# Output projection of a fused attention and gated-MLP kernel: where w_in is loaded, how many tiles are held, and which engine makes the low parts

## Chip, cores and metric

The kernel runs on one core of a Trainium2 chip, as one launch. The metric is the time of one execution on the device in microseconds (us). The time before is the median of three runs.

## What is computed

One transformer block in float32 for a sequence of 2048 rows with D = 448 features: an attention with 16 heads of 28 features, then a gated MLP that mixes along the sequence. Both have a layer norm ahead of them whose scale and shift come from a condition vector.

```python
mod = (_silu(c) @ w_mod).reshape(c.shape[0], 6, 1, -1)
sa, ca, ga, sb, cb, gb = ...
h = _layernorm(x) * (1 + ca) + sa
x = x + ga * _A_ref(h, A_wqkv, A_wo)          # softmax attention, then @ wo
h = _layernorm(x) * (1 + cb) + sb
x = x + gb * _B_ref(h, B_w_in, B_w_sp, B_b_sp, B_w_out)
# _B_ref: z = gelu(x @ w_in); z1, z2 = halves of z; z2 = layernorm(z2)
#         g = w_sp @ z2 + b_sp;  return (z1 * g) @ w_out
```

## The kernel before, in words

**Products from a high and a low part.** TensorE (PE) multiplies in float32r. A float32 operand is kept as a high part (a copy to float32r) and a low part (the operand less its high part). A product over 448 rows is eleven matmuls, in the order of `STEPS` (L27 to L29): nine `STEPS_MAIN` over the first 384 rows and two `STEPS_Z` over the last 64, whose high and low parts share slot 6. High parts are made by ScalarE (ACT) or GpSimd (POOL), low parts by `sub` (L70), a subtraction on VectorE (DVE) or POOL.

**The order is written by hand.** `tc.manual_schedule()` (L36) keeps each engine's instructions in the order of the source. Semaphores are put in for data and for the reuse of buffers. A DMA takes one of eight DMA semaphores in turn, and its issue also waits until the earlier DMA on that semaphore has landed. Most DMAs are issued by SyncE (SP).

**Stages.** (1) Norm of x, then q, k and v. q and k go to DRAM as high and low parts. (2) Attention over 256 positions u, 16 for each head (L550 to L562): at each position four score matmuls (`s_mm`, L419) of head u // 16, four matmuls for row maxima (`m_mm`, L388) that run 20 positions ahead, an exponential on ACT, a maximum on DVE, and P times V (`pv_mm`, L434) every second position. Head h reads its rows from the tiles k and q number h % 3 (`kst`, `qst`), which L324 to L329 place in the order k0, q0, q2, k2, q1, k1 with small pads between. Per head `n_copy` to `n_scatter` normalise the output and scatter it by DMA into `OT`, the transposed attention output in `heapD`; `o_split` (L477) splits it. (3) Output projection (L666 to L738), the stage that the change is about. (4) z1: 28 units of eleven matmuls (`z1_unit`, L714). (5) z2, the mixing along the sequence, and the product with w_out.

**The output projection.** `wo_mm` makes tile t (128 rows of the sequence, 16 tiles) of attention @ wo in one PSUM bank. `wo_add` adds it to x on DVE and stores the sum. The last head arrives late: after the last P times V, PE sums its softmax denominators, DVE takes the reciprocal (L680) and multiplies (L681), and eight DMAs scatter the result (L471, one row block and one column quarter each, half issued by SP and half by ACT). Then `o_split(3, qb)` splits column quarter qb of slot 6: ACT makes a high part `zt` (L486), DVE or POOL the low part (L71), ACT the high part in place (L488). Only `STEPS_Z` read slot 6. So PE first does `STEPS_MAIN` of `HELD` = 7 tiles, each held in one of the seven ring banks, and then their `STEPS_Z`. Tile t needs quarter t // 4.

For each group of four tiles follow `h2_stats` (statistics on DVE, `rstd_of` on POOL), `h2_norm` (eight DVE instructions, L638) and `h2_group`, which calls `ln_transpose`: 16 transposes on PE into four ring banks, and per bank two ACT passes (L111 into `hfull`, which has two buffers, and L118) and a low part on POOL (L71). The results, `h2T[g]`, are what z1 reads.

w_in's first half is loaded (L652, L74, L75) after the attention and split by `win_prep` into `w1`: the first two row blocks ahead of the held tiles' `STEPS_Z`, the others behind them, high parts on ACT and low parts on POOL. The x rows of group 0 are loaded ahead of the scatter, those of groups 1 to 3 behind it (L611).

Of the kernel before, what the change touches and what calls it, by code (L numbers as in the profile page):

```python
# [33 lines left out]
def tile_adaln_mha_gmlp(ctx, tc, x, wqkv, wo, w_in, w_spT, b_sp, w_out, cT, w_mod, out):  # L34
# [26 lines left out]
    heapD = dpool.tile([128, 24 * 896], F32R, name="heapD")  # L61
# [6 lines left out]
    wqk = hview(heapD, 14336, 8, 896)  # L68
# [8 lines left out]
    def weight_part(dst, i, raw, hi_eng, lo_eng, zero=True):  # L77

        n = raw.shape[-1]
        h = dst[:, i if i < 3 else 6, :n]  # L80
        if hi_eng is act:
            act.activation(h, raw, AF.Copy)
        else:
            hi_eng.tensor_copy(h, raw)
        if i < 3:
            sub(lo_eng, dst[:, 3 + i, :n], raw, h)
        else:
            sub(lo_eng, dst[0:64, 7, :n], raw[0:64], h[0:64])
            if zero:
                pool.memset(dst[64:128, 7, :n].bitcast(F32), 0.0)  # L90
# [6 lines left out]
    def ln_transpose(xns, full_pool, dsts, scol, bcol, engs, los=(pool,) * 4, mid=None, after=None):  # L97

        tps = []
        for c in range(4):  # L100
            tp = ring.tile([128, 512], F32, name="tp", tag="s")
            tps.append(tp)
            for t in range(4):
                pe.transpose(tp[:, t * 128 : (t + 1) * 128], xns[t][:, c * 128 : (c + 1) * 128], ident)  # L104
# [43 lines left out]

    def load_mod(pair, eng):
# [27 lines left out]
    pool.memset(wqk[64:128, 7, :].bitcast(F32), 0.0)  # L177
# [8 lines left out]
    wu = ring.tile([128, 512], F32, name="wu", tag="s")  # L186
# [16 lines left out]
    def mod_col(*parts):  # L203
        pc = ring.tile([128, 512], F32, name="pc", tag="s")
# [8 lines left out]
    def mod_bc(nm, acc):  # L213
        pc = ring.tile([128, 512], F32, name="pc", tag="s")
# [36 lines left out]
    def v_tiles(*kts):  # L251
        pvs = [ring.tile([128, 512], F32, name="pv", tag="s") for _ in kts]
# [7 lines left out]
    def qk_unit(m, g, mid=None):  # L260
        pq = ring.tile([128, 512], F32, name="pq", tag="s")
# [54 lines left out]
    for g in range(NG):  # L316
# [4 lines left out]
        if g == 3:  # L321
            early.close()
            stk = att.enter_context(tc.tile_pool(name="stk", bufs=1))
            kq = {}  # L324
# [60 lines left out]
    def m_mm(j, kb):  # L385
        h, t = divmod(j, NT)
        mt = ring.tile([128, 512], F32, name="mt", tag="s")
# [13 lines left out]
    def m_fin(h):  # L401
        mx = mxs.pop(h)
        tp = ring.tile([128, 512], F32, name="mtp", tag="s")
# [12 lines left out]
    def s_mm(u, qb):  # L416
        h, kt = divmod(u, NT)
        st = ring.tile([128, 512], F32, name="st_ps", tag="s")
# [43 lines left out]
    def n_scatter(h):  # L462
        o = osb.pop(h)
        a, e = h * DH, (h + 1) * DH
        while a < e:
# [3 lines left out]
            for qb in range(4):  # L469
                for (sl, r), eng in zip(dests, (sp, act if h == H - 1 else sp)):  # L470
                    eng.dma_start(  # L471
# [30 lines left out]

    LEAD = 20
# [21 lines left out]
    for i in range(4):  # L525
        at(120 + 8 * i, wo_load, i)
        at(124 + 8 * i, wo_prep, i)

# [44 lines left out]
    w2 = hview(heapD, 14336, 8, 896)  # L573
    uT = hview(heapD, 14336, 14, 512)
# [5 lines left out]
    wraw = fh.tile([128, 4, 896], F32, name="wraw", tag="heapE")  # L580
# [41 lines left out]
    def h2_stats(g):  # L622
        mv3[g] = t3.tile([128, 4, 2], F32, name="mv3"), t3.tile([128, 4], F32, name="rs3")
        sts = []
        for tt in range(4):
# [3 lines left out]
        for tt in range(4):  # L629
            dve.bn_aggr(out=mv3[g][0][:, tt, :], in_=sts[tt])  # L630
        rstd_of(mv3[g][0][:, :, 1], mv3[g][1], 4)

    def h2_norm(g):
        mv, rs = mv3.pop(g)
# [9 lines left out]
    def win_load(half, i, p=None):  # L644
        if half == 0:
            raw = wraw[:, i, :]
        else:
            raw = p.tile([128, 896], F32, name="raw_in", bufs=1)
        raw_in[half, i] = raw
        c0 = half * FH  # L650
        if i < 3:
            sp.dma_start(raw, w_in[i * 128 : (i + 1) * 128, c0 : c0 + FH])  # L652
        else:
            load_z(sp, raw, w_in[384:448, c0 : c0 + FH])

    def win_prep(half, i, lo_eng):
        weight_part((w1, w2)[half], i, raw_in.pop((half, i)), act, lo_eng)
# [6 lines left out]


# [5 lines left out]
    HELD = 7  # L671
    x_load(0)
    for i in range(4):
        win_load(0, i)
# [8 lines left out]
    for g in range(1, 4):  # L683
        x_load(g)
    for i in range(2):
        win_prep(0, i, pool)
    for t in range(1, HELD):
        wo_mm(t, STEPS_MAIN)
    for qb in range(4):
        o_split(3, qb, dve if qb % 2 == 0 else pool)  # L690
    for i in range(2, 4):
        win_prep(0, i, pool)
    for t in range(HELD):
        wo_mm(t, STEPS_Z)
        wo_add(t)
    h2_stats(0)
    wo_tile(7)
    h2_stats(1)
    h2_norm(0)
    stg.close()  # L700
# [4 lines left out]
    def h2_group(g):  # L705
# [4 lines left out]
        ln_transpose(xns, t3b, h2T[g], cols["cb"], cols["sb"], (act,) * 4)  # L710
# [3 lines left out]
    def z1_unit(g, f):  # L714
        ps_t = ring.tile([128, 512], F32, name="z1_ps", tag="s")
# [20 lines left out]
    h2_stats(3)  # L736
    win_load(1, 0, t3)
    win_load(1, 1, t3b)  # L738
    for g in range(NG):
        for f in range(7):  # L740
            z1_unit(g, f)
            if g == 0 and f == 0:
                h2_norm(3)
            if g == 0 and f in (1, 5):
                h2_group(2 + f // 5)
            if g == 1 and f in (3, 5):
                win_prep(1, f // 4, dve)
                win_load(1, 2 + f // 4, (t3, t3b)[f // 4])
# [23 lines left out]
    def z2_gemm(t):  # L772
# [3 lines left out]
        for hf in range(2):  # L776
            ps_t = ring.tile([128, 512], F32, name="z2_ps", tag="s")
# [42 lines left out]
    def mix_part(tb, st, f):  # L820
        hi, lo = wsp[tb, st]
        if st == 0:
            acc[f] = ring.tile([128, 512], F32, name="acc", tag="s")
# [118 lines left out]
```

## Time and profile before

| what | value |
|---|---|
| median of three runs (lowest to highest) | 1466.33 us (1465.02 to 1467.49) |
| time of the profiled execution | 1466.46 us |
| span of the profiled execution | 1464.7 us |
| granted TensorE clock, mean | 0.999 |
| first matmul of the output projection (L599) | 895.78 us |
| first matmul of z1 (L717) | 941.29 us |
| DMA, mean over the span | 76 GB/s |

Times within the profile are us from the start of the span. A row of the timeline has the start, the length, the engine, the line, the operation, its operands and the count of instructions merged into it; in brackets stands how long the engine was idle before it and what ended that. A row of the windows has, for each stretch, its length and the busy time and count of instructions on PE, PEld (weight loads), DVE, ACT and POOL, then the granted PE clock, the busy share of the DMA engines and their rate. A matmul's busy time is longer than its distance to the next one, because matmuls are pipelined: before a stall the last one is still shown as busy when PE could have issued the next.

### The profile page before, as it was taken

What the parts mean: (1) busy time and instruction counts of PE and PEld (TensorE: products, weight loads), DVE (VectorE), ACT (ScalarE), POOL (GpSimd) and SP (SyncE); (2) the same over time, 40 slices, a digit from 0 to 9 for tenths busy, and PEclk for the clock granted to TensorE, in tenths of its full rate; (3) what the DMA queues carried; (4) which work ended last, traced back from release to release, by engine and by line L of the source; (5) the groups of instructions that cost most, each with busy time, mean ns of one, the idle gap of its engine ahead of it and who ended that gap; (6) DMA issues with size and microseconds to landing.
All of it is one profiled execution on the core that took longest, in us unless ns stands there. A gap on an engine that the chain in (4) does not pass through costs nothing.

```text
span 1464.7 us, 19637 instructions
## 1 busy us (share of the span) xinstructions
PE 1436.5 (98%) x7314; PEld 1015.3 (69%) x7314; DVE 884.6 (60%) x1440; ACT 733.1 (50%) x1390; POOL 302.0 (21%) x273
## 2 busy tenths in 40 slices
PE   5899999999999999999999999999999999999999
PEld 5787755555555555555555555888988888888887
DVE  6557888888888888888888832921552411413114
ACT  3523577677677767767776786442432211211111
POOL 6734200000002011001000021520763400302002
PEclk9999999999999999999999999999999999999999
DMA  7554401221022211221012004442002321313223
GB/s 220 146 163 151 145 9 46 52 49 43 15 52 53 53 39 40 53 51 41 21 47 52 11 19 139 151 149 101 8 14 99 119 77 67 113 64 106 84 69 107
DMA packets 56133, 111.24 MB, mean 76 GB/s; under 512 B 11901, under 2 KB 22781, under 8 KB 53517
## 3 DMA queue, kind: packets, MB, share of 16 engines
q1 hardware_dynamic: 55868, 109.76, 25.1%
q8 instruction: 57, 0.93, 0.3%
q10 hardware_dynamic: 168, 0.23, 0.1%
q14 instruction: 40, 0.32, 0.1%
HBM read 75.89 MB, written 29.48 MB: 72 GB/s over the span
## 4 chain that ended last, share of the span: by engine, by line
PE 92%; DVE 2%; POOL 2%; DMA 2%; issue 1%; ACT 0%; SPq 0%; ACTq 0%; DVEq 0%; POOLq 0%
PE st_ps L419 18%; PE mt L388 16%; PE o_ps L434 16%; PE acc L825 7%; PE acc L827 7%; PE acc L826 7%; PE z_ps L779 5%; PE z_ps L717 5%; PE pq L265 4%; PE y_ps L866 2%; PE y_ps L865 2%; PE y_ps L867 2%; PE pv L256 1%; PE tp L104 1%; POOL heapD L71 1%
## 5 line engine op out<-in xcount | busy, mean ns | idle before, releaser
L393 DVE TENSOR_REDUCE pm<-mt 128x1 f32<-128x512 f32 x1024 | 632.0, 681 | 121.8 <-PE mt L388 121.4
L423 ACT ACTIVATE P<-st_ps 128x512 f32<-128x512 f32 x1024 | 514.2, 618 | 154.3 <-PE st_ps L419 153.9
L419 PE MATMUL st_ps<-qst,kst 86*128 86x512 f32 x1024 | 409.8, 411 | 0.0
L388 PE MATMUL mt<-kst,qst 84*128 84x512 f32 x1024 | 406.6, 397 | 0.3 <-DVE pm L393 0.3
L419 PEld LDWEIGHTS st_ps<-qst,kst 86*128 86x128 f32 x1024 | 193.1, 189 | 144.8 <-issue 82.2
L434 PE MATMUL o_ps<-P,V 128*32 128x512 f32 x2048 | 247.5, 598 | 0.0
L388 PEld LDWEIGHTS mt<-kst,qst 84*128 84x128 f32 x1024 | 194.8, 190 | 38.3 <-DVE pm L393 0.7
L71 DVE TENSOR_TENSOR wsp_l<-raw_sp,wsp_h 128x512 fp32r<-128x512 f32 x64 | 53.7, 841 | 185.7 <-ACT wsp_h L762 185.7
L762 ACT ACTIVATE wsp_h<-raw_sp 128x512 fp32r<-128x512 f32 x64 | 40.3, 631 | 229.1 <-DMA raw_sp<-in_w_spT_dram 187.3
L434 PEld LDWEIGHTS o_ps<-P,V 128*32 128x32 f32 x2048 | 54.1, 109 | 123.5 <-issue 116.6
L71 POOL TENSOR_TENSOR heapD<-u,heapD 128x512 fp32r<-128x512 f32 x27 | 44.7, 1692 | 254.0 <-ACT heapD L844 170.2
L460 POOL TENSOR_TENSOR osb<-osb,rb 128x512 f32<-128x512 f32 x15 | 19.2, 1281 | 349.6 <-DMA rb<-r_scr 192.0
L265 PE MATMUL pq<-heapD 128*128 128x512 f32 x308 | 85.8, 396 | 2.9 <-DVE heapD L71 2.9
L825 PE MATMUL acc<-wsp_h,heapD 128*128 128x512 f32 x224 | 87.6, 391 | 0.6 <-DVE u L842 0.6
L827 PE MATMUL acc<-wsp_h,heapD 128*128 128x512 f32 x224 | 87.3, 390 | 0.0
L826 PE MATMUL acc<-wsp_l,heapD 128*128 128x512 f32 x224 | 87.2, 389 | 0.0
L265 PEld LDWEIGHTS pq<-heapD 128*128 128x128 f32 x308 | 58.0, 189 | 16.4 <-DVE heapD L71 3.4
L71 POOL TENSOR_TENSOR nl<-nf,nh 16x128 fp32r<-16x128 f32 x16 | 7.2, 453 | 285.5 <-issue 152.3
L267 ACT ACTIVATE qf<-pq 128x512 f32<-128x512 f32 x28 | 16.7, 597 | 70.1 <-PE pq L265 70.1
L870 DVE TENSOR_TENSOR x2t<-x2t,y_ps 128x448 f32<-128x448 f32 x12 | 7.5, 622 | 72.9 <-PE y_ps L867 72.9
L825 PEld LDWEIGHTS acc<-wsp_h,heapD 128*128 128x128 f32 x224 | 42.1, 188 | 9.7 <-DVE u L842 1.4
L71 POOL TENSOR_TENSOR ql<-qf,qh 128x512 fp32r<-128x512 f32 x28 | 36.4, 1304 | 59.7 <-ACT qh L269 47.2
(150 smaller groups left out, 1693.3 us busy)
## 6 DMA issues: line engine op xcount, KB each, us to landing
raw_sp<-in_w_spT_dram SPq DMA_DIRECT2D x64, 256.0 KB
kst<-qk_scr SPq DMA_DIRECT2D x45, 224.0 KB
qst<-qk_scr SPq DMA_DIRECT2D x45, 224.0 KB
qk_scr<-qh SPq DMA_DIRECT2D x28, 256.0 KB
qk_scr<-ql SPq DMA_DIRECT2D x28, 256.0 KB
z_scr<-z1t SPq DMA_DIRECT2D x28, 256.0 KB
z<-z_scr SPq DMA_DIRECT2D x28, 256.0 KB
wm<-in_w_mod_dram SPq DMA_DIRECT2D x12, 392.0 KB
```

Of the source, the lines that this page charges most:

```text
L71: eng.tensor_tensor(out=dst, in0=a, in1=hi.bitcast(F32), op=ALU.subtract)
L265: pe.matmul(pq, wqk[:, b, m * 128 : (m + 1) * 128], hT[g][:, a, :], start=j == 0, stop=j == NST - 1)
L388: pe.matmul(mt, qst[h % 3][0:84, t * 128 : (t + 1) * 128], kst[h % 3][0:84, kb * 512 : (kb + 1) * 512], start=True, stop=True)
L393: dve.tensor_reduce(out=pms[h][:, t, kb : kb + 1], in_=mt, axis=AX.X, op=ALU.max)
L419: pe.matmul(st, kst[h % 3][0:86, kt * 128 : (kt + 1) * 128], qst[h % 3][0:86, qb * 512 : (qb + 1) * 512], start=True, stop=True)
L423: act.activation(p, st, AF.Exp, scale=SCALE)
L434: pe.matmul(otile[h][32 * qb : 32 * qb + 32, :], V[:, kt, h, :], ptiles.pop((u, qb)), start=kt == 0, stop=kt == NT - 1)
L717: pe.matmul(ps_t, w1[:, b, f * 128 : (f + 1) * 128], h2T[g][:, a, :], start=j == 0, stop=j == NST - 1)
L779: pe.matmul(ps_t[:, :D], h2T[g][:, a, tt * 128 : (tt + 1) * 128], w2[:, b, hf * D : (hf + 1) * D], start=j == 0, stop=j == NST - 1)
L825: pe.matmul(acc[f], z2[st][:, 0, fs], hi, start=st == 0, stop=False)
L826: pe.matmul(acc[f], z2[st][:, 0, fs], lo, start=False, stop=False)
L827: pe.matmul(acc[f], z2[st][:, 1, fs], hi, start=False, stop=st == NT - 1)
```

## The change

1. **w_in's first half is loaded during attention.** `heapD` is cut into 20 rows and a separate tile `heapF` of 4 rows at the same address. `heapF` first holds the upper half of `wqk`, then `wraw` (the raw w_in), then the upper halves of `w2` and `uT` (class `Halves`). The loads are issued at positions 180, 188, 196 and 204. All four `win_prep` stand ahead of the held tiles, and all four x loads ahead of the scatter.
2. **Eight held tiles.** Tile 7 (and 15) takes the bank of `ps_o` in place of a ring bank.
3. **The last splits on DVE**, all four, two of them between the adds; three of the eight scatters are issued by ACT and five by SP.
4. **Order after the splits.** Tiles 8 to 12 come before the first group's transposes, 13 and 14 between the two groups, 15 after the second. The low parts of all four groups are on DVE in place of POOL. The third group's four statistics stand between the second group's low parts. Groups 2 and 3 follow the 5th and the 10th z1 unit (they followed the 2nd and the 6th).
5. **k and q tiles** are placed in the order k0, q0, k1, q1, k2, q2 without pads. By the built program their first bytes lie in the partition at 54336, 62528, 70784 (q2), 78976 (k2), 87200 (q1) and 95424 (k1) before, and at 54080 and each 8192 bytes on after.

`bank(...)` is the ring allocation under a shorter name, and `:n` became `0:n`; neither changes an instruction.

```diff
-    heapD = dpool.tile([128, 24 * 896], F32R, name="heapD")
+    heapD = dpool.tile([128, 20 * 896], F32R, name="heapD")
+    heapF = dpool.tile([128, 4 * 896], F32R, name="heapF", tag="heapF")
...
-            for i, (nm, pad) in enumerate((("k0", 64), ("q0", 0), ("q2", 16), ("k2", 0), ("q1", 8), ("k1", 8))):
-                if pad:
-                    stk.tile([128, pad], F32, name=f"pad{i}")
-                kq[nm] = stk.tile([128, S], F32R, name=f"{nm[0]}st{nm[1]}")
-            kst, qst = ([kq[f"{n}{i}"] for i in range(3)] for n in "kq")
+            kq = [[stk.tile([128, S], F32R, name=f"{n}st{i}") for n in "kq"] for i in range(3)]
+            kst, qst = [a[0] for a in kq], [a[1] for a in kq]
...
-                for (sl, r), eng in zip(dests, (sp, act if h == H - 1 else sp)):
-                    eng.dma_start(
+                for (sl, r), i in zip(dests, (2 * qb, 2 * qb + 1)):
+                    (act if h == H - 1 and i in (1, 3, 6) else sp).dma_start(
...
+        at(180 + 8 * i, win_first, i)
...
-            wo_ps[t] = ring.tile([128, 512], F32, name="wo_ps", tag="s")
+            wo_ps[t] = bank("wo_ps") if t % 8 < 7 else ps_o.tile([128, 512], F32, name="wo_ps", tag="o")
...
-    HELD = 7
-    x_load(0)
+    HELD = 8
+    for g in range(4):
+        x_load(g)
     for i in range(4):
-        win_load(0, i)
+        raw_in[0, i] = wraw[0][:, i, :]
+        win_prep(0, i, pool)
...
-    for g in range(1, 4):
-        x_load(g)
-    for i in range(2):
-        win_prep(0, i, pool)
     for t in range(1, HELD):
         wo_mm(t, STEPS_MAIN)
-    for qb in range(4):
-        o_split(3, qb, dve if qb % 2 == 0 else pool)
-    for i in range(2, 4):
-        win_prep(0, i, pool)
-    for t in range(HELD):
+    o_split(3, 0, dve)
+    o_split(3, 1, dve)
+    for t in range(4):
         wo_mm(t, STEPS_Z)
         wo_add(t)
+    o_split(3, 2, dve)
+    for t in range(4, 8):
+        wo_mm(t, STEPS_Z)
+        wo_add(t)
+    o_split(3, 3, dve)
     h2_stats(0)
-    wo_tile(7)
     h2_stats(1)
     h2_norm(0)
...
-        ln_transpose(xns, t3b, h2T[g], cols["cb"], cols["sb"], (act,) * 4)
+        ln_transpose(xns, t3b, h2T[g], cols["cb"], cols["sb"], (act,) * 4, (dve,) * 4, None, after)
...
-    for t in (8, 9, 10):
+    for t in range(8, 12):
         wo_tile(t)
     h2_norm(1)
-    wo_tile(11)
-    h2_group(0)
-    h2_stats(2)
-    wo_tile(12)
-    wo_tile(13)
+    wo_mm(12, STEPS)
+    wo_add(12)
+    h2_group(0, lambda c: wo_tile(13) if c == 2 else None)
+    wo_tile(14)
+
+    def last_tile(c):
+        if c == 2:
+            wo_tile(15)
+        h2_stats(2, ((0, 2, 1, 3).index(c),))
+
+    h2_group(1, last_tile)
     h2_norm(2)
-    h2_group(1)
-    wo_tile(14)
-    wo_tile(15)
     h2_stats(3)
...
-            if g == 0 and f == 0:
+            if g == 0 and f == 4:
+                h2_group(2)
                 h2_norm(3)
-            if g == 0 and f in (1, 5):
-                h2_group(2 + f // 5)
+            if g == 1 and f == 2:
+                h2_group(3)
```

More of the change, by code (lines that the diff above doesn't have):

```diff
@@ L100, in ln_transpose @@
         for c in range(4):
-            tp = ring.tile([128, 512], F32, name="tp", tag="s")
+            tp = bank("tp")
             tps.append(tp)
@@ L147, in tile_adaln_mha_gmlp, with bank @@
     wms, xts, raws = {}, {}, {}
+    def bank(name):
+        return ring.tile([128, 512], F32, name=name, tag="s")
     def load_mod(pair, eng):
@@ L251, in v_tiles @@
     def v_tiles(*kts):
-        pvs = [ring.tile([128, 512], F32, name="pv", tag="s") for _ in kts]
+        pvs = [bank("pv") for _ in kts]
         for j, (a, b) in enumerate(STEPS):
@@ L386, in m_mm @@
         h, t = divmod(j, NT)
-        mt = ring.tile([128, 512], F32, name="mt", tag="s")
+        mt = bank("mt")
         pe.matmul(
@@ L501, in wo_prep, with win_first @@
         weight_part(wos, i, wo_raw.pop(i), pool, pool)
+    wraw = []
+    def win_first(i):
+        if not wraw:
+            wraw.append(dpool.tile([128, 4, 896], F32, name="wraw", tag="heapF"))
+        if i < 3:
+            sp.dma_start(wraw[0][:, i, :], w_in[i * 128 : (i + 1) * 128, 0:FH])
+        else:
+            load_z(sp, wraw[0][:, 3, :], w_in[384:448, 0:FH])
     LEAD = 20
@@ L620, in wo_add, with h2_stats @@
         sp.dma_start(x2_scr[t * 128 : (t + 1) * 128, :], xt[:, :D])
[L622 to L625, printed above, removed]
+    def h2_stats(g, tts=range(4)):
+        if g not in mv3:
+            mv3[g] = t3.tile([128, 4, 2], F32, name="mv3"), t3.tile([128, 4], F32, name="rs3"), []
+        mv, rs, sts = mv3[g]
+        for tt in tts:
             st = t3.tile([128, 6], F32, name="st3", bufs=4)
```

77 lines of the change are left out of this document (39 added, 38 removed).

## Prediction, made before the changed kernel ran

> **What bounds the kernel now.** I read the page first, then the windows of the stage between attention and z1, then the timeline of PE in it, and last the rows of whatever ended PE's waits.
>
> ```profile
> PE 92%; DVE 2%; POOL 2%; DMA 2%; issue 1%; ACT 0%; SPq 0%; ACTq 0%; DVEq 0%; POOLq 0%
> ```
>
> The chain that ended last is PE for 92% of the span. PE's own matmuls therefore set the time, and an edit helps only where PE waits or where its matmuls come faster.
>
> ```profile
> 895.78:910.00 14.22, 14.10 (x66) 12.13 (x65) 4.70 (x3) 3.56 (x6) 1.97 (x1) 1.00 0.74 223
> 910.00:914.50 4.50, 1.96 (x9) 1.50 (x9) 3.46 (x5) 2.38 (x5) 4.29 (x3) 1.00 0.81 274
> ...
> 926.70:941.30 14.60, 13.05 (x79) 11.86 (x78) 13.91 (x24) 8.49 (x13) 8.07 (x8) 1.00 0.26 95
> 941.30:1015.10 73.80, 73.80 (x342) 61.35 (x341) 19.79 (x29) 33.56 (x52) 15.95 (x14) 1.00 0.36 128
> ```
>
> PE is idle only between 910 and 914.5 (2.54 of 4.50 us) and between 926.7 and 941.3 (1.55 us). From 941.3 on, in z1, it has no gap. The timeline shows the stops one by one:
>
> ```profile
> 898.16 11.72 PE L599 MATMUL wo_ps<-heapD 128*128 128x448 f32 x54
> 910.80 1.88 PE L599 MATMUL wo_ps<-heapD 128*128 128x448 f32 x8 [0.92 <-ACT zt L486]
> 914.42 12.63 PE L599 MATMUL wo_ps<-heapD 128*128 128x448 f32 x61 [1.74 <-POOL heapD L71]
> 926.89 1.91 PE L104 MATMUL tp<-ident,x 128*128 128x128 f32 x16
> ...
> 933.10 0.79 PE L104 MATMUL tp<-ident,x 128*128 128x128 f32 x3
> 935.35 1.64 PE L104 MATMUL tp<-ident,x 128*128 128x128 f32 x13 [1.46 <-DVE x L638]
> 936.75 4.71 PE L599 MATMUL wo_ps<-heapD 128*128 128x448 f32 x22
> 941.29 1.07 PE L717 MATMUL z_ps<-heapB,heapA 128*128 128x512 f32 x4
> ```
>
> Pace: 61 matmuls begin between 914.42 and 926.89, so one takes 0.204 us. Thirteen transposes begin between 935.35 and 936.75, so one takes 0.108 us. With these, PE could have gone on at 898.16 + 54 x 0.204 = 909.18, at 910.80 + 8 x 0.204 = 912.43 and at 933.10 + 3 x 0.108 = 933.42. It went on at 910.80, 914.42 and 935.35. The stops cost 1.62 + 1.99 + 1.93 = **5.5 us**. That is all this stage can give.
>
> **The change part by part.** The first two stops are the wait for the last splits:
>
> ```profile
> 902.23 0.69 DVE L681 TENSOR_TENSOR osb<-osb,rb 128x512 f32<-128x512 f32 x1
> 902.95 3.94 ACTq L471 DMA_DIRECT2D heapD<-osb  x4
> ...
> 907.00 1.80 ACT L82 ACTIVATE heapA<-wraw 128x896 fp32r<-128x896 f32 x2 [10.47 <-DMA heapD<-osb]
> 908.03 4.65 POOL L71 TENSOR_TENSOR heapA<-wraw,heapA 128x896 fp32r<-128x896 f32 x2 [32.86 <-DMA heapD<-osb]
> 908.70 0.61 ACT L486 ACTIVATE zt<-heapD 128x512 fp32r<-128x512 f32 x1
> 909.35 1.35 DVE L71 TENSOR_TENSOR heapD<-heapD,zt 64x512 fp32r<-64x512 f32 x1 [6.43 <-ACT zt L486]
> ...
> 912.76 1.60 POOL L71 TENSOR_TENSOR heapD<-heapD,zt 64x512 fp32r<-64x512 f32 x1
> ```
>
> The second quarter's low part stood on POOL behind two of w1's (until 912.68) and ended at 914.36. In the new order it is on DVE, and w1's work is earlier: ACT's four high parts follow the copy of the last head's output (0.90 us each, from 896.6), POOL's four low parts run from 897.5 at about 2.1 us each, to 906 with the memset.
>
> The price is one collision. DVE's multiply at 902.23 now meets POOL's third low part (901.7 to 903.8). Rows of before show what follows: DVE's low part at 909.35 took 1.35 us on 64 partitions beside POOL, where the multiply took 0.69 us on 128 with POOL idle. So the multiply ends between 902.9 and 904.6, and I take 904.6. The Trainium skill ("SBUF — State Buffer", section "SBUF: two separate sides") calls this an exclusive lock: a DVE instruction with two SBUF inputs waits out a POOL instruction that reads SBUF. The trace agrees: the 1.35 us ended 0.5 us after POOL's first low part. By that rule alone the scatter leaves 1.7 us later, which speaks against the change.
>
> Loading w_in early does not empty the queue ahead of the scatter:
>
> ```profile
> x<-in_x_dram SPq DMA_DIRECT2D x3, 896.0 KB
> ...
> wraw<-in_w_in_dram SPq DMA_DIRECT2D x3, 448.0 KB
> ```
>
> Before, one x load and four row blocks of w_in were ahead (2688 KB, 2.75 MB). After, it is four x loads (3584 KB, 3.67 MB).
>
> ```profile
> 897.60:904.00 6.40, 6.40 (x31) 5.42 (x30) 4.05 (x2) 0.00 (x0) 0.00 (x0) 1.00 1.01 373
> ```
>
> At 373 GB/s from 897.6 the x loads end at 907.4. SP's five scatters follow in the same queue, and three of them wait for the landing of an x load by their semaphores. Before, the first split began 908.70 - 902.95 = 5.75 us after the first issue, partly behind ACT's w1 work. I put the first split at 908.5 to 910.3 and take 909.5. ACT needs 1.2 us for a quarter (0.61 + 0.63), DVE 0.7 us behind the high part. So quarter 0 is ready at 910.8 and quarter 1 at 912.0.
>
> PE has 63 matmuls of held tiles after 898.16 (nine more than before) and reaches `STEPS_Z` at 911.0. Tiles 0 to 3 take 1.6 us, and tile 4 needs quarter 1 at 912.6. So no wait with the value taken, 0.8 us with the first split at 910.3. Both stops (3.6 us) go. Next late is DVE:
>
> ```profile
> 913.26 3.81 DVE L619 TENSOR_TENSOR x<-x,wo_ps 128x448 f32<-128x448 f32 x7
> 916.99 2.20 DVE L627 BATCH_NORM_STATS2 st<-x 128x6 f32<-128x448 f32 x4
> 919.11 0.36 DVE L630 BATCH_NORM_AGGREGATE mv<-st 128x2 f32<-128x6 f32 x4
> ...
> 923.26 3.19 DVE L638 TENSOR_SCALAR x<-x,mv,rs 128x64 f32<-128x64 f32 x8 [0.89 <-POOL rs L95]
> ...
> 927.96 7.34 DVE L638 TENSOR_SCALAR x<-x,mv,rs 128x64 f32<-128x64 f32 x8
> ```
>
> From 911.7 its order is: four adds at 0.54 (2.2), a split (0.7), four adds (2.2), a split (0.7), two statistics (2 x 2.56), a norm (3.19). That ends at 925.8, or 926.2 if the first add is 0.4 late. PE arrives at 898.16 + 134 x 0.204 = 925.5. New wait: 0.3 to 0.7 us, I take **0.5**.
>
> The third stop (1.93) was the second norm, which took 7.34 us beside POOL's low parts against 3.19 us without. With the low parts on DVE, POOL has none here, so I take 3.19. DVE: adds of 8 to 11 until 928.4, norm until 931.6, add 12 until 932.2, then the first low part at 0.69, until 932.9. PE: transposes until 927.9, tiles 13 and 14 until 932.4, then transposes again. Their third bank was ACT's third pass of group 0, whose buffer that first low part frees:
>
> ```profile
> 927.59 0.78 ACT L111 ACTIVATE hfull<-tp,col_sb,col_cb 128x512 f32<-128x512 f32 x1 [10.20 <-PE tp L104]
> 928.40 0.63 ACT L118 ACTIVATE heapB<-hfull 128x512 fp32r<-128x512 f32 x1
> ```
>
> 932.9 + 0.78 = 933.7 against PE's 933.3: new wait 0.4 us. If the low parts cost 1.4 us, as beside POOL, it is 1.1 us. I take **0.7**. Group 0's last low part ends near 936.3, before PE's 937.2. Later DVE has the third group's norm done at about 947.5, where PE, after five z1 units (2.5 us each by the last window above), asks at 949.7. So the later place of groups 2 and 3 costs nothing; without those 2 us it would cost what is missing.
>
> Taken at nothing: the four w_in loads during attention (1.84 MB, 5 us at 373 GB/s, spread over 70 us in which the DMA share is about 0.2, below; if a load holds up m's DMA, that one has ten us to spare). `uT` and `w2` keep their addresses.
>
> **The k and q tiles.** The attention has 64 score matmuls in each of these three stretches, one head each (heads 3, 4 and 5):
>
> ```profile
> 305.73:352.29 46.56, 46.56 (x259) 26.80 (x258) 39.34 (x68) 33.15 (x68) 1.74 (x2) 1.00 0.18 42
> 352.29:398.98 46.69, 46.69 (x258) 26.80 (x257) 39.31 (x68) 33.22 (x69) 1.74 (x2) 1.00 0.17 41
> 398.98:445.48 46.50, 46.50 (x258) 26.70 (x257) 39.29 (x67) 33.12 (x68) 7.27 (x8) 1.00 0.18 42
> ```
>
> PE has no gap in any, yet they differ by up to 0.19 us. The work is the same; the tiles differ. So the place of the tiles may set a few ns per matmul, which no row shows directly. If all 14 full heads ran as the third, 14 x (46.58 - 46.50) = 1.2 us would be gained; if all ran as the second, 14 x 0.11 = 1.5 us lost. Addresses not seen here could go further. I take **0** and keep -3 to +4.
>
> **Sum.** 5.5 us of stops go, 0.5 + 0.7 and 0.2 for the splits come: 1466.46 - 4.1 = 1462.4 us. The median shown is 0.13 below the profiled execution, which gives 1462.3 us.
>
> **Rivals.** (a) *The wait moves to DVE.* Eight low parts join it between 932 and 943. For it: it is busy 13.91 of 14.60 us already. Against: 7.34 us of that is a norm stretched by POOL. If low parts stay at 1.4 us and the norm at 5 us, PE's second transposes start 2 us late: gain 2, 1464.3 us. (b) *The scatter is held by the x loads.* At 274 GB/s (910 to 914.5 above) they end at 911, quarter 0 is ready at 914, PE waits 3 us: gain 1.1, 1465.2 us. Against: the 373 GB/s were on the same queue. (c) *Attention runs faster* with all six tiles at one offset, by 2 us more than nothing: 1460.3 us. (d) *Attention runs slower.* Place: the score and maximum matmuls of 15 heads. Slower than before by over 0.2% needs 4.1 + 2.9 = 7 us, or 0.47 us a head: it decides from 47.05 us a head on, and at 47.1 us (8.2 us) gives 1470.5 us. Against: that is more than twice the spread seen. (e) *It does not do what it says*: w1 still runs when the splits come, and both stops stay: gain 1.9 less 1.2, 1465.6 us. Against: nothing holds ACT's high parts behind the scatter now.
>
> **How the numbers follow.** Forecast 0.47; (a) 0.13; (b) 0.08; (c) 0.17; (d) 0.10; (e) 0.05. The range reaches from (c) with a full gain of 5.5, 1466.3 - 5.5 - 2 = 1458.8, to just over no change, 1467.5, past (a), (b) and (e); only (d) and the far end of (c) stay out. Differences under 0.2%, 2.9 us, can hardly be told from none: faster means below 1463.4. The forecast and its neighbours toward losses of 1 us and more in attention give: faster 0.56, same 0.33, slower 0.11.
>
> **What would show it.** Right: z1's first matmul about 41.4 us after the output projection's first (45.51 before), no idle PE row at the first `STEPS_Z`, short stops of 0.3 to 0.7 us at each group's transposes, the second norm near 3.2 us, and head stretches of 46.4 to 46.8 us. Wrong: a multiply at 902 that takes over 2.5 us, a first `zt` later than 15 us after the first projection matmul, low parts on DVE of 1.3 us and more, or heads at 47 us.

## Result and profile after

The changed kernel takes 1460.75 us (median of 12 runs, 1459.44 to 1465.07). The kernel before, run on the same chip, takes 1465.62 us. The ratio is 0.9969, with a 95% interval of 0.996 to 0.9979. So 4.9 us are gained, where 4.0 had been forecast (1462.3 against 1466.33), and the time lies inside the range of 1458.8 to 1467.5.

The profiled execution after takes 1460.85 us, with a span of 1459.1 us. These are the rows of its timeline that answer to those of before: start, length, engine, line, and in brackets the idle time ahead and what ended it.

```profile
893.39 2.09 PE L618 MATMUL wo_ps<-heapD 128*128 128x448 f32 x9
...
895.06 8.78 POOL L83 TENSOR_TENSOR heapA<-wraw,heapA 128x896 fp32r<-128x896 f32 x4 [22.30 <-ACT heapA L94]
895.77 13.58 PE L618 MATMUL wo_ps<-heapD 128*128 128x448 f32 x63
899.84 2.04 DVE L699 TENSOR_TENSOR osb<-osb,rb 128x512 f32<-128x512 f32 x1
901.90 7.30 SPq L482 DMA_DIRECT2D heapD<-osb  x5
901.90 3.34 ACTq L482 DMA_DIRECT2D heapD<-osb  x3
...
908.54 0.63 ACT L497 ACTIVATE zt<-heapD 128x512 fp32r<-128x512 f32 x1 [11.04 <-DMA heapD<-osb]
910.00 14.63 PE L618 MATMUL wo_ps<-heapD 128*128 128x448 f32 x71 [0.65 <-ACT heapD L499]
...
921.81 3.16 DVE L659 TENSOR_SCALAR x<-x,mv,rs 128x64 f32<-128x64 f32 x8
924.47 2.41 PE L116 MATMUL tp<-ident,x 128*128 128x128 f32 x16
926.64 4.71 PE L618 MATMUL wo_ps<-heapD 128*128 128x448 f32 x22
927.01 3.19 DVE L659 TENSOR_SCALAR x<-x,mv,rs 128x64 f32<-128x64 f32 x8
930.64 1.29 DVE L83 TENSOR_TENSOR heapB<-hfull,heapB 128x512 fp32r<-128x512 f32 x2
931.19 1.91 PE L116 MATMUL tp<-ident,x 128*128 128x128 f32 x16
...
932.85 2.48 PE L618 MATMUL wo_ps<-heapD 128*128 128x448 f32 x11
935.16 1.09 PE L736 MATMUL z_ps<-heapB,heapA 128*128 128x512 f32 x4
```

Read it from the bottom. z1 begins at 935.16, 41.77 us after the first projection matmul at 893.39; before it was 45.51. The stage gave 3.7 us. Of the three stops, one is left, ahead of the first `STEPS_Z` at 910.00. It ends with the splits, whose first instruction, the first `zt`, began at 908.54, 15.15 us behind the stage's start, and had waited for the scatter ("DMA heapD<-osb"). The second norm takes 3.19 us where it took 7.34. DVE's low parts take 0.65 us each (two in 1.29).

The two spans differ by 5.6 us, and not all of that is the change. This table has every profile of the study: the start of the first score matmul, the attention (from there to the first projection matmul), the stage (from there to z1), and the first `zt` behind the stage's start, all in us. The kernel before, next to each, ran on the same chip.

| profile | first score | attention | stage | first zt | median (before) |
|---|---|---|---|---|---|
| before | 167.14 | 728.64 | 45.51 | 12.92 | |
| after | 165.62 | 727.77 | 41.77 | 15.15 | 1460.75 (1465.62) |
| e12_after_again | 166.84 | 727.47 | 41.88 | 15.27 | 1461.82 (1466.29) |
| e1_kq | 165.24 | 727.00 | 45.36 | 12.81 | 1465.17 (1465.53) |
| e6_old_kq | 165.52 | 728.12 | 40.87 | 13.62 | 1461.94 (1466.46) |
| e2_low_pool | 166.84 | 727.17 | 45.72 | 14.92 | 1465.09 (1465.53) |
| e3_mult | 164.14 | 727.34 | 41.75 | 15.15 | 1460.65 (1465.53) |
| e4_x | 164.14 | 727.39 | 40.66 | 12.03 | 1459.52 (1465.53) |
| e11_x_again | 165.37 | 727.77 | 40.14 | 12.04 | 1461.26 (1466.29) |
| e5_x_held7 | 165.20 | 727.49 | 40.66 | 12.03 | 1459.63, one run |
| e8_win_late | 167.82 | 727.18 | 47.75 | 17.20 | 1465.54 (1466.46) |
| e9_held7 | 167.04 | 727.12 | 41.65 | 13.73 | 1462.38 (1466.46) |
| e7_split_pool | 165.10 | 727.43 | 41.42 | 15.05 | 1459.50 (1466.46) |
| e10_stats | 167.81 | 727.73 | 41.42 | 14.82 | 1462.65, one run |

No edit here changes the work ahead of the first score, yet that part spreads from 164.14 to 167.82. The part behind z1's start spreads from 523.4 to 525.2. The same code spreads too: the two profiles of the kernel after differ by 1.22 us ahead of the first score and by 1.0 us behind z1's start. Both spreads are larger than most effects here. Behind z1's start the change moved groups 2 and 3; that shows nothing clear of this spread (523.4 and 525.0 in before and e1_kq, 523.9 and 524.9 in after and e12_after_again). So each edit is read in its own stretch, and the medians serve as a check. What is left of the change: 3.7 us in the stage and, by the mean of the twelve profiles with the new tile order (727.40) against the two with the old (728.38), 1.0 us in the attention. Together 4.7, against 4.9 by the medians.

### The profile page after: what moved, and what is told of

The parts are those of the page before. It is cut to its first block, busy times and chain, and to the rows that moved or that the text cites. A ratio compares the mean times of both kernels' runs of the same rounds, so it can differ in the third digit from the quotient of the medians.

```text
span 1459.1 us, 19621 instructions
## 1 busy us (share of the span) xinstructions
PE 1436.4 (98%) x7314; PEld 1017.5 (70%) x7314; DVE 881.3 (60%) x1458; ACT 732.4 (50%) x1390; POOL 276.3 (19%) x255
## 4 chain that ended last, share of the span: by engine, by line
PE 94%; DVE 3%; DMA 2%; issue 1%; SPq 0%; ACT 0%; POOL 0%; DVEq 0%; ACTq 0%
PE st_ps L430 18%; PE mt L399 16%; PE o_ps L445 16%; PE acc L848 6%; PE acc L850 6%; PE acc L849 6%; PE pq L280 5%; PE z_ps L802 5%; PE z_ps L736 5%; PE pv L271 2%; PE y_ps L889 2%; PE y_ps L888 2%; PE y_ps L890 2%; PE tp L116 1%; PE wo_ps L618 1%
## 5 line engine op out<-in xcount | busy, mean ns | idle before, releaser
L83 POOL TENSOR_TENSOR heapF<-u,heapD 128x512 fp32r<-128x512 f32 x27 | 44.6, 1684 | 256.8 <-ACT heapD L867 256.8
L280 PE MATMUL pq<-heapD 128*128 128x512 f32 x196 | 64.6, 407 | 0.0
L848 PEld LDWEIGHTS acc<-wsp_h,heapD 128*128 128x128 f32 x224 | 42.1, 188 | 10.5 <-DVE u L865 2.3
L850 PEld LDWEIGHTS acc<-wsp_h,heapD 128*128 128x128 f32 x224 | 42.1, 188 | 8.9
L849 PEld LDWEIGHTS acc<-wsp_l,heapD 128*128 128x128 f32 x224 | 42.1, 188 | 8.2
```

The source lines that it names most:

```text
L83: eng.tensor_tensor(out=dst, in0=a, in1=hi.bitcast(F32), op=ALU.subtract)
L280: pe.matmul(pq, wqk[:, b, m * 128 : (m + 1) * 128], hT[g][:, a, :], start=j == 0, stop=j == NST - 1)
L848: pe.matmul(acc[f], z2[st][:, 0, fs], hi, start=st == 0, stop=False)
L849: pe.matmul(acc[f], z2[st][:, 0, fs], lo, start=False, stop=False)
L850: pe.matmul(acc[f], z2[st][:, 1, fs], hi, start=False, stop=st == NT - 1)
```

## Experiments

### Where the k and q tiles lie: e1_kq and e6_old_kq

e1_kq is the kernel before with the new order alone; e6_old_kq is the kernel after with the old order.

```diff
-            kq = {}
-            for i, (nm, pad) in enumerate((("k0", 64), ("q0", 0), ("q2", 16), ("k2", 0), ("q1", 8), ("k1", 8))):
...
+            kq = [[stk.tile([128, S], F32R, name=f"{n}st{i}") for n in "kq"] for i in range(3)]
```

> The kernel before with one part of the change alone: the k and q tiles of attention allocated in their natural order and without the pads between them. In the profiles of before and after, attention (first score matmul to first projection matmul) took 728.64 and 727.77 us, heads 46.50 to 46.73 by head mod 3 before and 46.47 to 46.68 after. Theory: the addresses of these tiles set that difference, so attention takes about 727.8 us here and the time falls by 0.9 us, to about 1464.7. Rival: the addresses do nothing, attention stays at 728.6 within 0.2, the heads keep their pattern by head mod 3, and the time is that of before within 1 us. The idle PE row of 3.0 us at 70.12, which before shows and after does not, tells apart as well: if it is there again, it belongs to the code, if it isn't, to the single execution.

> The kernel after with the k and q tiles of attention back in the order and with the pads of before, the converse of e1_kq. There the natural order alone gave attention (first score matmul to first projection matmul) 727.00 us against before's 728.64, while four profiles with the change's layout gave 727.2 to 727.8. Theory: the addresses of these tiles set attention, so it takes 728.3 to 728.9 us here, with heads that differ by head mod 3, and the time is 1.0 to 1.6 us over after's. Rival: what sets it is another part of the layout or the execution itself: attention stays at 727.0 to 727.8. The projection stage stays at 41.8 by either.

The windows of heads 3, 4 and 5 in e1_kq (length of the stretch, busy time and count on PE, PEld, DVE, ACT and POOL, granted clock, DMA share, GB/s):

```profile
303.45:349.93 46.48, 46.48 (x259) 26.72 (x257) 39.30 (x67) 33.15 (x68) 1.73 (x2) 1.00 0.18 42
349.93:396.41 46.48, 46.48 (x259) 26.72 (x257) 39.30 (x67) 33.15 (x68) 1.73 (x2) 1.00 0.18 42
396.41:442.87 46.46, 46.46 (x258) 26.67 (x257) 39.30 (x68) 33.16 (x68) 7.27 (x8) 1.00 0.18 42
```

The same heads in e6_old_kq:

```profile
303.94:350.45 46.51, 46.51 (x258) 26.80 (x257) 39.30 (x67) 33.12 (x68) 1.73 (x2) 1.00 0.18 42
350.45:397.16 46.71, 46.71 (x258) 26.77 (x257) 39.32 (x68) 33.20 (x69) 1.73 (x2) 1.00 0.18 41
397.16:443.62 46.46, 46.46 (x258) 26.70 (x257) 39.29 (x67) 33.12 (x68) 7.24 (x8) 1.00 0.18 42
```

With the new order the three heads are alike; with the old one the head that works on k1 and q1 is 0.2 us longer, as before. All profiles show it: the heads that work on k1 and q1 (1, 4, 7, 10 and 13) take 46.70 to 46.79 us in the two with the old order and 46.46 to 46.57 in the twelve with the new one. Undoing this one edit brings the pattern back, and applying it alone removes it. So the addresses set it, at about 1 us over the attention (1.6 in e1_kq; 0.7 in e6_old_kq against the mean, less than expected). This is 0.07% of the time, and the interval of e1_kq's ratio, 0.9979 to 1.0002 around 0.999, holds it without showing it. Why an address costs PE 0.2 us in the 258 matmuls of such a head is not settled. The stage of e6_old_kq had been expected at 41.8 and took 40.87, because its scatter landed earlier (below).

### What sets the scatter: e3_mult, e4_x and e11_x_again

e3_mult (the first diff) takes two low parts off POOL while DVE multiplies; e4_x (the second) takes two x loads out of the scatter's way; e11_x_again is e4_x once more.

```diff
-    for i in range(4):
+    for i in range(2):
         raw_in[0, i] = wraw[0][:, i, :]
         win_prep(0, i, pool)
+    for i in range(2, 4):
+        act.activation(w1[:, 2 if i < 3 else 6, :], wraw[0][:, i, :], AF.Copy)
+    pool.memset(w1[64:128, 7, :].bitcast(F32), 0.0)
...
     n_scatter(h)
+    sub(dve, w1[:, 5, :], wraw[0][:, 2, :], w1[:, 2, :])
+    sub(dve, w1[0:64, 7, :], wraw[0][0:64, 3, :], w1[0:64, 6, :])
```

```diff
-    for g in range(4):
+    for g in range(2):
         x_load(g)
...
     n_scatter(h)
+    for g in range(2, 4):
+        x_load(g)
```

> The kernel after, with w1's third and fourth low parts on DVE behind the last head's multiply, so that POOL has done its two when the multiply starts. It takes away what lengthened the multiply (2.04 us after, 0.69 before), not the loads of x ahead of the scatter. Theory A, the multiply sets the scatter: the scatter is issued 1.35 us earlier, the first zt starts at about 13.8 us after the first projection matmul in place of 15.15, PE's stop of 1.38 us ahead of the first STEPS_Z falls to 0.0 to 0.1, and the time falls by 1.3 us. Theory B, the four loads of x fill the DMA engines until about 906.5 and set the scatter: it is issued 1.35 us earlier but lands less than 0.5 us earlier, the stop stays at 0.9 to 1.4 and the time within 0.5 us of after.

> The kernel after, with the loads of x's third and fourth group issued behind the last head's scatter. It takes away the transfers that the scatter shares the DMA engines with, not the length of the multiply. Theory B (loads of x set the scatter's landing): the scatter issued at about 8.5 us after the first projection matmul lands about 2 us behind its issue, the first zt starts at 11.5 to 13 us in place of 15.15, PE's stop of 1.38 us ahead of the first STEPS_Z goes and the time falls by about 1.3 us. Theory A (the multiply sets it): the first zt starts no more than 0.4 us earlier, and the time stays within 0.4 us of after. The tiles of the third group could be late instead: then PE stops at the ninth tile's sum or its bank, at about 28 us.

> e4_x once more, beside the kernel after on the same chip, as the fastest version so far. Theory: the stage takes 40.66 us whatever the transfers do, against 40.7 to 41.8 after (a mean of about 41.4 from the profiles with four loads ahead), so it is 0.5 to 1 us faster than after, within what the early part varies by. Rival: nothing, since the landing mostly comes in time after as well: within 0.3 us.

The timeline of e3_mult, whose stage begins at 891.48:

```profile
897.92 0.69 DVE L702 TENSOR_TENSOR osb<-osb,rb 128x512 f32<-128x512 f32 x1
898.64 8.24 SPq L482 DMA_DIRECT2D heapD<-osb  x5
...
906.63 0.63 ACT L497 ACTIVATE zt<-heapD 128x512 fp32r<-128x512 f32 x1 [11.03 <-DMA heapD<-osb]
908.08 14.62 PE L618 MATMUL wo_ps<-heapD 128*128 128x448 f32 x71 [0.65 <-ACT heapD L499]
```

The multiply is back at 0.69 us and the scatter leaves 1.35 us earlier, 7.16 us into the stage in place of 8.51. The first `zt` still comes at 15.15. The stage is unchanged, 41.75. That is theory B. The timeline of e4_x, whose stage begins at 891.53:

```profile
893.91 28.25 PE L618 MATMUL wo_ps<-heapD 128*128 128x448 f32 x134
897.98 2.04 DVE L699 TENSOR_TENSOR osb<-osb,rb 128x512 f32<-128x512 f32 x1
900.04 4.22 SPq L482 DMA_DIRECT2D heapD<-osb  x5
903.56 0.63 ACT L497 ACTIVATE zt<-heapD 128x512 fp32r<-128x512 f32 x1 [7.91 <-DMA heapD<-osb]
```

Here the multiply is as long as in after, and the scatter leaves at the same 8.51 us. It lands in half the time: `zt` 3.5 us behind the issue in place of 6.6. PE runs all 134 matmuls without a stop. The two kernels part the causes: with four loads ahead, the transfers ahead of the scatter set its landing and the multiply does not. The DMA engines show it as well: in after they are busy for a share of 0.96 and more from 3 to 13 us into the stage, in e4_x the share is down to 0.12 from 7 to 8 us, before the scatter is issued. Another path could be the semaphores that scatters share with x loads, but in after seven of the eight issues follow one another within 3.4 us (8.51 to 11.85), and only the last waits, until 15.07.

On the whole time the repetition gave 1461.26 us, 0.6 below the kernel after on the same chip (ratios to before 0.9964, 0.9951 to 0.9978, and 0.9967, 0.9955 to 0.998). The stage is 1.1 to 1.7 us shorter, but no comparison of medians here can show that, and up to 0.5 of it is PE's pace (last section).

### What the eighth tile covers: e9_held7 and e5_x_held7

e9_held7 is the kernel after with this edit; e5_x_held7 has this edit and that of e4_x.

```diff
-    HELD = 8
+    HELD = 7
...
     for t in range(4, 8):
-        wo_mm(t, STEPS_Z)
+        wo_mm(t, STEPS_Z if t < 7 else STEPS)
```

> The kernel after with seven held tiles in place of eight: the eighth tile's nine main matmuls come behind the splits. Theory: each held tile covers 1.84 us (nine matmuls of 0.204) of the wait for the scatter, so PE's stop ahead of the first STEPS_Z grows from 1.38 to 3.2 us and the stage from 41.8 to 43.6. Rival: the held tile is not the cover, since the same work is done later and some later stop shrinks by it: the stage grows by less than 0.8 us.

> e4_x (the third and fourth x load behind the scatter) with seven held tiles in place of eight. In e4_x the first zt began 12.0 us after the first projection matmul, PE had no stop and the stage took 40.66 us; in e9_held7, with all x loads ahead, the first zt began 13.7 us after it, and PE reached the first STEPS_Z 13.5 us after it and stopped 1.6 us. Theory: what counts is the landing alone: with the split ready 1.45 us behind the zt, at 13.5, seven tiles cover it and the stage is 40.7 to 40.9 us, so that the eighth held tile is a second cure for the same wait. Rival: the eighth tile does more than cover the landing (its bank, or the order of the adds on DVE): the stage is 41.2 us or more, with a stop of 0.4 us or more somewhere behind the splits.

The timeline of e9_held7:

```profile
896.58 11.51 PE L618 MATMUL wo_ps<-heapD 128*128 128x448 f32 x54
...
907.90 0.63 ACT L497 ACTIVATE zt<-heapD 128x512 fp32r<-128x512 f32 x1 [9.62 <-DMA heapD<-osb]
909.35 16.45 PE L618 MATMUL wo_ps<-heapD 128*128 128x448 f32 x80 [1.26 <-DVE heapD L83]
```

The timeline of e6_old_kq, with eight tiles:

```profile
896.02 28.25 PE L622 MATMUL wo_ps<-heapD 128*128 128x448 f32 x134
907.26 0.63 ACT L501 ACTIVATE zt<-heapD 128x512 fp32r<-128x512 f32 x1 [9.51 <-DMA heapD<-osb]
```

These two had nearly the same landing (13.73 and 13.62 us), earlier than after's. With eight tiles PE does not stop; with seven it does, from 896.58 + 54 x 0.204 = 907.60 to 909.35, 1.75 us (1.43 by the two matmul starts around it). So the eighth tile covered at least 1.4 us; the 1.84 of the theory fits, but is not shown. The stop of 3.2 us and the stage of 43.6 were missed, because the landing came 1.4 us earlier than in after. Against after's 41.77 the stage of 41.65 is even what the rival said, so the cover shows only beside e6_old_kq, which had the same landing: 41.65 is 0.8 longer than 40.87, and not 1.4, since PE ran at 203 ns a matmul where e6_old_kq ran at 207 (last section). With two x loads out of the way, e5_x_held7 (one execution) needs no eighth tile: 40.66, no stop, as with eight. The tile and the order of the loads are two cures for one wait.

### Loading w_in early: e8_win_late

```diff
-        at(180 + 8 * i, win_first, i)
...
-    for g in range(4):
-        x_load(g)
+    x_load(0)
+    for i in range(4):
+        win_first(i)
...
     n_scatter(h)
+    for g in range(1, 4):
+        x_load(g)
```

> The kernel after with w_in's first half loaded behind attention as before (behind the first group of x), and x's other three groups behind the last head's scatter as before: the early load alone undone. e4_x showed that the scatter's landing hangs on the transfers ahead of it: with 3.67 MB the first zt came 15.15 us after the first projection matmul, with 1.83 MB 12.0. Here 2.75 MB lie ahead. Theory: they end about 7 to 7.5 us behind their first byte, the scatter lands 12 to 13.3 us after the first projection matmul, no stop is left ahead of the first STEPS_Z, and the stage takes 40.6 to 41.0 us, less than after: the early load bought nothing that the order of x's loads did not take back. Rival: w1's copies on ACT and low parts on POOL come only when w_in has landed, so they meet the multiply or the splits on DVE (each 2 us in place of 0.69): the first zt stays at 14 to 16 us and the stage at 41.8 to 43.

Its timeline, in a stage that begins at 895.00:

```profile
906.53 0.95 ACT L94 ACTIVATE heapA<-wraw 128x896 fp32r<-128x896 f32 x1 [0.50 <-DMA wraw<-in_w_in_dram]
906.56 3.29 ACTq L482 DMA_DIRECT2D heapD<-osb  x3
...
912.19 0.63 ACT L497 ACTIVATE zt<-heapD 128x512 fp32r<-128x512 f32 x1 [4.70 <-DMA heapD<-osb]
913.64 2.36 PE L617 MATMUL wo_ps<-heapD 128*128 128x448 f32 x8 [2.69 <-DVE heapD L83]
917.34 15.18 PE L617 MATMUL wo_ps<-heapD 128*128 128x448 f32 x63 [1.34 <-DVE heapD L83]
```

Its window behind the second stop:

```profile
917.30:921.70 4.40, 4.36 (x12) 3.91 (x13) 4.34 (x8) 2.18 (x4) 0.00 (x0) 0.51 0.56 211
```

The theory is refuted, and the rival named another wait and too small a price; the multiply took 0.69 us here. Less was queued ahead of the scatter, but ACT keeps the order of the source: its copies of w_in waited for their loads until 906.53, and its three scatter issues stood behind them. The stage is 47.75, 6.0 us over after. Two stops make some 3.7 us of it (by matmul starts 2.85 and 1.7, less the 0.8 that after has). The rest is the clock: in the window it was granted at 0.51, and twelve matmuls took 4.40 us. So the early load is what lets `win_prep` stand ahead of the scatter; that place without it costs 6 us.

### Which engine makes the low parts and splits: e2_low_pool and e7_split_pool

```diff
-        ln_transpose(xns, t3b, h2T[g], cols["cb"], cols["sb"], (act,) * 4, (dve,) * 4, None, after)
+        ln_transpose(xns, t3b, h2T[g], cols["cb"], cols["sb"], (act,) * 4, (pool,) * 4, None, after)
```

```diff
-    o_split(3, 1, dve)
+    o_split(3, 1, pool)
...
-    o_split(3, 3, dve)
+    o_split(3, 3, pool)
```

> The kernel after, with the low parts of the transposed groups (h2_group) back on POOL. Theory: POOL's low parts hold the shared port against the second group's normalization on DVE, whose eight operations took 7.34 us before and 3.19 after; so they take about 7 us again, a PE stop of about 1.9 us comes back before the second group's transposes or the matmuls behind them, and the time rises by 1.5 to 2.0 us over after, to about 1462.5. Rival: the tiles now placed between the transposes cover the longer normalization; it is 7 us long again, but PE does not stop and the time stays within 0.4 us of after.

> The kernel after with the second and fourth split of the last slice back on POOL. Theory: POOL is free since w1's last low part (903.9 in after), so its split, about 1.2 us where DVE's is 0.69, ends about 0.6 us later, still ahead of the matmul that needs it (four tiles' STEPS_Z, 1.6 us, lie between); the stage stays at 41.8 within 0.3, and what took before's second split stop of 1.99 us away was the emptied POOL, not DVE. Rival: POOL's and DVE's splits hold each other on the shared port, the split takes 2 us or more, PE stops ahead of the fifth tile's STEPS_Z for 0.7 to 2 us and the stage is 42.5 to 43.8.

The timeline of e2_low_pool, and below it a window of the stretch from its last row here:

```profile
927.30 2.63 POOL L83 TENSOR_TENSOR heapB<-hfull,heapB 128x512 fp32r<-128x512 f32 x2 [3.37 <-PE tp L116]
927.40 7.20 DVE L659 TENSOR_SCALAR x<-x,mv,rs 128x64 f32<-128x64 f32 x8
...
930.15 2.66 POOL L83 TENSOR_TENSOR heapB<-hfull,heapB 128x512 fp32r<-128x512 f32 x2 [0.22 <-ACT heapB L130]
...
933.11 0.33 PE L116 MATMUL tp<-ident,x 128*128 128x128 f32 x1 [1.27 <-DVE x L659]
933.89 0.33 PE L116 MATMUL tp<-ident,x 128*128 128x128 f32 x1 [0.45 <-DVE x L659]
934.66 3.01 PE L116 MATMUL tp<-ident,x 128*128 128x128 f32 x13 [0.44 <-DVE x L659]
```

```profile
934.66:937.34 2.68, 2.68 (x13) 2.68 (x14) 2.07 (x4) 1.81 (x3) 0.53 (x1) 0.50 0.50 187
```

The norm is long again beside POOL, as the theory said, but the stage loses 3.95 us, twice the 1.5 to 2.0 of the theory: 45.72, as long as before the change. PE waits for the norm's tiles one by one, and then its clock is granted at 0.50: thirteen transposes take 2.68 us where before's thirteen took 1.40. That is 1.3 us for the clock and the rest for the waits. So, in the new order, the low parts on DVE are worth as much as the stage gained in all. The order leaves less room for a long norm: with the low parts on POOL the second group's transposes begin 4.2 us behind the start of their norm (931.56 against 927.40), where in before they began 5.1 us behind it (933.10 against 927.96).

e7_split_pool changes nothing. Its split on POOL, in the timeline:

```profile
909.47 1.30 POOL L83 TENSOR_TENSOR heapD<-heapD,zt 64x512 fp32r<-64x512 f32 x1 [5.59 <-ACT zt L497]
```

1.30 us, with no idle row on PE behind it and a stage of 41.42. So the second split's stop of before came from POOL's other work, which the change had moved away, and not from the engine.

### The third group's statistics: e10_stats

```diff
-        h2_stats(2, ((0, 2, 1, 3).index(c),))
...
+    h2_stats(2)
     h2_group(1, last_tile)
```

> The kernel after with the third group's four statistics on DVE ahead of the second group's transposes and low parts, in place of one behind each low part. Theory: DVE has room, since z1 asks for the second group only after seven units (17.5 us): the second group's low parts come 2.5 us later, nothing waits for them, and the stage stays at 40.7 to 41.8 us (by when the first zt comes), z1 without a stop. Rival: the lows of the second group hold ACT's passes back (hfull has two buffers), ACT's first gelu comes 2.5 us later and the ring of banks runs out: PE stops in z1 for 0.3 to 2 us.

```profile
936.96 12.67 PE L736 MATMUL z_ps<-heapB,heapA 128*128 128x512 f32 x55
949.46 1.91 PE L116 MATMUL tp<-ident,x 128*128 128x128 f32 x16
```

In this timeline z1 has no idle row. ACT's pass waits 1.71 us for DVE and the first gelu comes later, but PE does not notice. The stage, 41.42, is in the range of after's. Where the statistics stand is worth nothing that shows in this one execution.

### The kernel after once more: e12_after_again

> The kernel after, unchanged, once more. Theory: the first zt comes at one of two times, about 13.7 us (as in e6_old_kq and e9_held7) or about 15.1 us (as in after, e2_low_pool, e3_mult and e7_split_pool) after the first projection matmul, whatever the code, and the stage is 40.7 or 41.8 us accordingly; attention takes 727.0 to 727.8 us. Rival: the two times belong to the kernels: 15.1 and 41.8 again. The first score matmul, 165.6 in after, may be anywhere between 164 and 168 as in the other profiles.

```profile
909.58 0.63 ACT L497 ACTIVATE zt<-heapD 128x512 fp32r<-128x512 f32 x1 [11.16 <-DMA heapD<-osb]
...
911.04 14.91 PE L618 MATMUL wo_ps<-heapD 128*128 128x448 f32 x71 [0.77 <-ACT heapD L499]
```

In a stage that begins at 894.31 this is 15.27 us, and the stage takes 41.88. It came out as the rival says. All six profiles with four x loads ahead, eight held tiles and the new place of the k and q tiles lie at 14.8 to 15.3 (after, e12_after_again, e2_low_pool, e3_mult, e7_split_pool, e10_stats); e6_old_kq and e9_held7, with the same loads ahead, at 13.6 to 13.7. Whether that is chance or code stays open. It is not the bulk of the transfers: in e6_old_kq the last packet of the x loads ends at 14.4 us into the stage, later than in after (13.6), while the last one of ACT's scatters ends at 13.6 there and at 15.15 in after. A few late packets decide.

## Why the prediction was right, step by step

- **The stops that could go**: right. The stage ran in 40.1 to 40.9 us wherever no stop was left, 4.6 to 5.4 under before's 45.5, against the 5.5 of the working. That figure counts a little too much: single matmul starts show 0.40 us behind the sums of the denominators in every profile, and a pace of 203 or 207 ns. By the two starts around each, the stops of before were 1.08, 1.90 and 1.93 us, 4.9 in all, which leaves 40.6.
- **The split stops (0.2 us left)**: the mis-sized term. By the working's own rule 895.77 + 63 x 0.204 = 908.62 to 910.00, 1.38 us; by the two starts around it 1.02 in place of 0.21 us, 0.8. The first `zt` had been taken at 13.7 us into the stage and came at 15.15.
- **The multiply beside POOL**: right, and worth nothing. It took 2.04 us in place of 0.69 and ended near where taken (8.49 us into the stage, 8.82 taken), 0.55 us after POOL's third low part (901.87 against 901.32). The Trainium skill ("SBUF — State Buffer", section "SBUF: two separate sides") has the lock, and the row agrees. That the scatter leaves later for it speaks against the change only where the scatter is then free to land; e3_mult shows that with four loads ahead it was not.
- **The x loads ahead of the scatter**: the right mechanism, rival (b), at part of its price: a stop of 0.8 us (1.4 by the working's rule) in place of 3. e4_x shows it.
- **The first norm (0.5)**: 924.47 + 16 x 0.108 = 926.20 against 926.64, 0.44. Right here; the other profiles with DVE's low parts show 0 to 0.44.
- **The third bank (0.7)**: 0. The first low part began at 930.64 and the transposes at 931.19; 16 of them took 1.66 us, at 0.104 each. Into the stage, the low part began at 37.25 us (36.4 in the working) and the transposes at 37.8 (36.6), so the transposes came 1.2 us later and the low part 0.85. That is 0.35 us of room, as much as the working's own wait of 0.4; the rest of the 0.7 was a margin that the low parts, 0.65 us each, did not need.
- **The second norm**: 3.19 us, as taken. That POOL stretched it is shown by e2_low_pool; its price there, 3.95 us, was not foreseen.
- **Early loads of w_in at nothing**: right in the attention. The loads fall into heads 11 and 12, which took 46.52 and 46.62 us in after and 46.48 and 46.63 in e8_win_late without them. That they are needed, by 6 us in this order, was not seen.
- **The k and q tiles at 0**: about -1.0. The bound from the fastest head, -1.2, had been the better value, and rival (c) was the right mechanism at half its size.

By the working's own terms the stage closes: 5.5 less 1.4 for the splits, 0.4 for the first norm and 0 for the third bank is 3.7, as measured. It was forecast at 41.4 and took 41.8, because a split term that was 1.2 too small and a bank term that was 0.7 too large nearly cancel; the attention, taken at 0, brought what takes the sum from 4.1 to 4.7. So the mechanisms were right, and that the total came this close is partly luck. (One sum in the rivals is a little off, and nothing rests on it: 47.1 us a head is 15 x 0.52 = 7.8 us more, not 8.2.)

## What to carry to other kernels

The wait for a small DMA was shortened here by moving the transfers ahead of it, and not by making it leave sooner: test both, since one alone can be worth nothing. Undo each part of a change singly, and also ask which parts need each other, as the early load and the early copies do here. Where the whole time varies by 2 us between executions, read an edit of 1 us in its own stretch, between two marks of the trace.

## What the hardware showed beside this

**A stop can cost more than its length.** In e8_win_late the lowered clock added some 2 us to two stops, in e2_low_pool 1.3 us to three short waits. Whether the clock falls can change from one execution to the next. The windows behind PE's stop of 2.92 us (before) and 2.95 us (after) at the same place in the first stage, first before:

```profile
38.32:42.90 4.58, 4.58 (x20) 3.81 (x21) 2.34 (x8) 3.01 (x5) 4.05 (x5) 1.00 0.25 62
```

and after:

```profile
38.87:44.16 5.29, 5.29 (x13) 4.18 (x14) 2.34 (x8) 3.10 (x5) 4.75 (x5) 0.50 0.20 50
```

Once the clock stays at 1.00, once it is granted at 0.50 over the 5.3 us shown, and thirteen matmuls take longer than twenty. The Trainium skill ("TensorE: Matmul & The Clock Gate", section "Part 1: The HAM clock gate") says that the window that decides is 3.4 us long and free-running, so that the same stop may or may not meet it. The traces agree with that: in all fourteen the granted clock changes on a grid of 3.41 us, and the grid parts before's stop into 1.8 and 1.1 us and after's into 2.1 and 0.8. That rule of the Trainium skill speaks of a whole idle window; here less is enough. Where the clock stood at 1.00, it fell behind every grid step in which PE was idle for 2.1 us or more (fifteen cases) and stayed behind all with up to 1.8 us, but for one: e2_low_pool's fell at 934.10, behind waits of 1.27 and 0.45 us with single transposes between.

In the first stage the drop did not make the first score later. The four profiles in which the clock stayed up there (before, e8_win_late, e9_held7, e10_stats) have a second stop of 3.0 to 3.1 us at about 67 us and their first score at 167.0 to 167.8; in the other ten, e1_kq among them, that stop is 1.1 us or less, and the first score comes at 164.1 to 166.8. So the stop that e1_kq's expectation asked about belongs to the execution, not to the code.

**Two paces of PE.** Between stops the projection's matmuls start on average either 203 or 207 ns apart at a granted clock of 1.00, and keep to one of the two over a stretch. In e11_x_again it is 203 for 134 of them, in e4_x, the same code, 207:

```profile
895.55 27.72 PE L618 MATMUL wo_ps<-heapD 128*128 128x448 f32 x134
```

27.72 us against 28.25, which is the 0.5 us between their stages. In after it went from 207 to 203 at the stop. What sets the pace was not tried.
